# Attention and soft mixture of experts: nine output rows per partition, all stores on one queue, DMA tiles placed first in SBUF

## Chip, cores, metric

The kernel runs on one core of one Trainium2 chip. The metric is the time of one execution on the device in microseconds (us), as a median over several runs. The rows of this output are nearly alike (in the reference, an element differs from the mean of its column by under 1% of its size on average), so the comparison with the reference hardly notices rows in wrong places.

## The reference, cut to what matters

```
# attention: 8 batches, 8 heads, 576 positions, 64 per head; causal window of 64
attn = softmax(mask(q @ k.T / 8)) @ v
x    = attn as [4608, 512]                    # row = 576 * batch + position
# soft mixture of experts: 8 experts, 4 slots each, F = 1024
logits = x @ phi                              # [4608, 32]
slot_in = softmax over rows(logits).T @ x     # [32, 512]
slot_out[e] = relu(slot_in[e] @ w1[e]) @ w2[e]
out = softmax over slots(logits) @ slot_out   # [4608, 512] fp32, 9.44 MB
```

## The kernel before: the parts that matter here

Inputs (q, k, v, then the experts' weights, 61.9 MB of fp32) are loaded in one long stream, all but the first block from the POOL queue, which converts them to fp16. Attention follows it block by block. For every row the exponentials of its 32 logits are kept in `ET`. At the end a small matmul per 128 rows (`combine`) multiplies `ET` by the experts' output `slot_oa`; ScalarE and VectorE (ACT and DVE) divide by the row's sum and move the result from PSUM (the memory that matmuls write) into a tile `ob` in SBUF (the memory that DMAs load and store); a DMA stores it. In the profiles PE is the matmul engine, PEld its loads of the stationary operand ("weight loads"), and SP and POOL are two more engines whose queues issue DMAs.

The last two experts' second weights (`w2`) come as two halves of columns, so that the first half of the output columns can be computed and stored ("half-width" stores, 256 columns) while the second half of those weights is still under way. The rows after those go out at full width (512 columns).

Two facts about `combine` are important. 576 rows per batch are 4 chunks of 128 and 64 left over, and the left-over rows of two batches share one chunk of 128 partitions. Their rows lie far apart in memory, so they are stored by two DMAs of 64 partitions. And a normal store takes each partition's row of 512 fp32, so it moves runs of 2 KB (1 KB at half width).

```
    # SBUF pools, in order of allocation (cut)
    const = ...; pld = ...; pqt; ppm; psm; pxb; pxt
    gap.tile([128, 64], FP16, name="gap")          # a filler of 128 bytes
    pw1 = ...(bufs=8)                              # w1, later the output tiles "ob"
    pw2 = ...(bufs=7); pet = ...
    ...
    ET = const.tile([128, 4 * B + B // 2, 128], FP16, name="ET")   # 36 chunks of 128 rows
    ...
    def combine(blk, cols):
        nd = cols.stop - cols.start
        ob = pw1.tile([128, 4, nd], FP32, name="ob", tag="w1s")
        for g in range(4):
            cp = ps2.tile([128, nd], FP32, name="cp", tag="cp", bufs=4)
            nc.tensor.matmul(cp[:, :], ET[:, 4 * blk + g, :], slot_oa[:, cols], start=True, stop=True)
            ...                                    # scale by 1/row sum: ACT for even g, DVE for odd g
        if blk < B:
            for g in range(0, 4, 2):
                nc.sync.dma_start(                 # SP queue, 128 partitions
                    out=out[S * blk + 128 * g:S * blk + 128 * g + 256, cols].rearrange("(c p) d -> p c d", p=128),
                    in_=ob[:, g:g + 2, :])
        else:                                      # the left-over rows, 64 partitions each
            for o in range(2):
                (nc.gpsimd, nc.scalar)[o].dma_start(
                    out=out.rearrange("(c o t) d -> o t c d", o=2, t=S)[o, 512:576, :, cols],
                    in_=ob[64 * o:64 * o + 64, :, :])
    ...
        slots_out(0)
        for blk in range(NSPLIT): combine(blk, halves[0])      # NSPLIT = 4
        for e in last: expert_o(e, 1)
        slots_out(1)
        for blk in range(NSPLIT): combine(blk, halves[1])
        for blk in [B] + list(range(NSPLIT, B)): combine(blk, whole)
```

The softmax here doesn't subtract the row's maximum and nothing guards it: scores larger than these inputs give would overflow.

Of the kernel before, what the change touches and what calls it, by code (L numbers as in the profile page):

```python
# [8 lines left out]
FP32 = mybir.dt.float32  # L9
FP16 = mybir.dt.float16  # L10
AF = mybir.ActivationFunctionType
ALU = mybir.AluOpType
AXX = mybir.AxisListType.X
# [3 lines left out]
def kernel(  # L17
# [10 lines left out]
    nc = tc.nc  # L28

    B, H, S, Dh = q.shape  # L30
    D, NSLOT = moe_phi.shape
    E, _, F = moe_w1.shape
    SPE = NSLOT // E
    T = 9
# [3 lines left out]
    NFC = F // 128  # L38
    scale = 1.0 / float(Dh) ** 0.5

    const = ctx.enter_context(tc.tile_pool(name="const", bufs=1))
    pld = ctx.enter_context(tc.tile_pool(name="pld", bufs=3))
    pqt = ctx.enter_context(tc.tile_pool(name="pqt", bufs=2))
    ppm = ctx.enter_context(tc.tile_pool(name="ppm", bufs=2))
    psm = ctx.enter_context(tc.tile_pool(name="psm", bufs=4))
    pxb = ctx.enter_context(tc.tile_pool(name="pxb", bufs=2))
    pxt = ctx.enter_context(tc.tile_pool(name="pxt", bufs=1))
    gap = ctx.enter_context(tc.tile_pool(name="gap", bufs=1))
    gap.tile([128, 64], FP16, name="gap")
    pw1 = ctx.enter_context(tc.tile_pool(name="pw1", bufs=8))  # L50
    pw2 = ctx.enter_context(tc.tile_pool(name="pw2", bufs=7))
    pet = ctx.enter_context(tc.tile_pool(name="pet", bufs=2))


# [57 lines left out]
    ident = const.tile([128, 128], FP16, name="ident")  # L112
# [13 lines left out]
    for h in range(2):  # L126
        nc.vector.tensor_copy(
            out=rep[64 * h:64 * h + 64, :, :],
            in_=ident[64 * h:64 * h + 64, 64 * h:64 * h + 64].unsqueeze(1).broadcast_to([64, 8, 64]))
# [19 lines left out]
    nc.gpsimd.dma_start(out=phi_sb, in_=moe_phi.rearrange("(c p) s -> p c s", p=128))  # L149
    phi4 = const.tile([128, NHD, 4, NSLOT], FP16, name="phi4")  # L150

    ET = const.tile([128, 4 * B + B // 2, 128], FP16, name="ET")
    crcp = const.tile([128, B, 5], FP32, name="crcp")
    acc = const.tile([128, D], FP32, name="acc")
    esum = const.tile([128, B + B // 2 + 1], FP32, name="esum")
    slot_inT = const.tile([128, NHD, NSLOT], FP16, name="slot_inT")
    slot_oa = const.tile([128, D], FP16, name="slot_oa")
# [127 lines left out]
    def moe_chunks(b):  # L285
        c = [4 * (b % 2) + i for i in range(4)]
        return c + [8] if b % 2 else c
# [21 lines left out]
    fin = {}  # L309
# [59 lines left out]
                             start=(kk == 0), stop=(kk == NHD - 1))  # L369

    def fin_et(b, part):
        ch = et_chunks(b)[2 * part:2 * part + 2]
        col = (b, B + B // 2, B + b // 2)[part]
        nc.scalar.activation(ET[:, ch[0]:ch[0] + len(ch), :], fin["lt", part].rearrange("p (c q) -> p c q", q=128),
                             AF.Exp, accum_out=esum[:, col:col + 1])

    def fin_rows(b):
        rs = psm.tile([128, 5], FP32, name="rs", tag="rs")
        nc.vector.reduce_sum(rs[:, :], fin["ex"][:, :, :], axis=AXX)
        nc.vector.reciprocal(crcp[:, b, :], rs[:, :])  # L380

    def stage_logit(b):

        lt = ps.tile([128, 512], FP32, name="lt", tag="tr", bufs=4)
        for kk in range(NHD):
            nc.tensor.matmul(lt[:, :], phi4[:, kk].rearrange("p r s -> p (r s)"), moe[b][:, kk],  # L386
                             start=(kk == 0), stop=(kk == NHD - 1))
        nc.scalar.activation(ET[:, 4 * b:4 * b + 4, :], lt[:, :].rearrange("p (c q) -> p c q", q=128),
                             AF.Exp, accum_out=esum[:, b:b + 1])
        if b % 2:  # L390
            l8 = ps.tile([128, 128], FP32, name="l8", tag="tr", bufs=4)
            for kk in range(NHD):
                nc.tensor.matmul(l8[:, :], phi4[:, kk].rearrange("p r s -> p (r s)"), moe[b, 8][:, kk],
                                 start=(kk == 0), stop=(kk == NHD - 1))
            nc.scalar.activation(ET[:, 4 * B + b // 2, :], l8[:, :], AF.Exp,
                                 accum_out=esum[:, B + b // 2:B + b // 2 + 1])

    def et_chunks(b):
        return [4 * b + n for n in range(4)] + ([4 * B + b // 2] if b % 2 else [])

    def stage_ex(b):

        ch = et_chunks(b)
        nch = len(ch)
        te = ps.tile([128, 5, NSLOT], FP32, name="te", tag="tr", bufs=4)
        for n, c in enumerate(ch):
            nc.tensor.matmul(te[:, n, :], ET[:, c, :], ident[:, 0:NSLOT], start=True, stop=True)
        ex = psm.tile([128, 5, NSLOT], FP16, name="ex", tag="ex", bufs=2)
        nc.scalar.copy(out=ex[:, 0:nch, :], in_=te[:, 0:nch, :])
        rs = psm.tile([128, 5], FP32, name="rs", tag="rs")  # L410
        nc.vector.reduce_sum(rs[:, 0:nch], te[:, 0:nch, :], axis=AXX)
        nc.vector.reciprocal(crcp[:, b, 0:nch], rs[:, 0:nch])
        moe["ex", b] = ex

    def stage_slot(b):
# [37 lines left out]
    for u in range(nu):  # L453
# [4 lines left out]
        for j in range(3):  # L458
# [9 lines left out]
            if pend is not None:  # L468
# [5 lines left out]
                if pj == 2 and units[pu][1] == 1:  # L474
                    b = units[pu][0]
# [7 lines left out]
    b = B - 1  # L483
# [20 lines left out]
    ps2 = ctx.enter_context(tc.tile_pool(name="ps2", bufs=2, space=bass.MemoryType.PSUM, reuse_waits="tile"))  # L504
# [27 lines left out]
    halves = (slice(0, D // 2), slice(D // 2, D))  # L532

    def expert_o(e, half):
        hT = hTs[e % NLAST]
        for i in range(NFC // 4):
            for g in range(4):
                nc.tensor.matmul(sop[half][32 * g:32 * g + 32, :], hT[:, 4 * i + g, :],
                                 w2_t[e][:, 4 * i + g, halves[half]],
                                 start=(e == 0 and i == 0), stop=(e == E - 1 and i == NFC // 4 - 1))  # L540

    def slots_out(half):
        if half == 0:
            nc.scalar.copy(out=slot_oa[:, halves[half]], in_=sop[half])
        else:
            nc.vector.tensor_copy(out=slot_oa[:, halves[half]], in_=sop[half])


    def combine(blk, cols):
        nd = cols.stop - cols.start  # L550
        ob = pw1.tile([128, 4, nd], FP32, name="ob", tag="w1s")
        for g in range(4):
            cp = ps2.tile([128, nd], FP32, name="cp", tag="cp", bufs=4)
            nc.tensor.matmul(cp[:, :], ET[:, 4 * blk + g, :], slot_oa[:, cols], start=True, stop=True)  # L554
            cr = crcp[:, blk, g:g + 1] if blk < B else crcp[:, 2 * g + 1, 4:5]
            if g % 2 == 0:
                nc.scalar.activation(ob[:, g, :], cp[:, :], AF.Copy, scale=cr)  # L557
            else:
                nc.vector.tensor_scalar(out=ob[:, g, :], in0=cp[:, :], scalar1=cr, scalar2=None, op0=ALU.mult)  # L559
        if blk < B:  # L560
            for g in range(0, 4, 2):
                nc.sync.dma_start(
                    out=out[S * blk + 128 * g:S * blk + 128 * g + 256, cols].rearrange("(c p) d -> p c d", p=128),
                    in_=ob[:, g:g + 2, :])
        else:
            for o in range(2):
                (nc.gpsimd, nc.scalar)[o].dma_start(
                    out=out.rearrange("(c o t) d -> o t c d", o=2, t=S)[o, 512:576, :, cols],
                    in_=ob[64 * o:64 * o + 64, :, :])

    NSPLIT = 4
    whole = slice(0, D)
    with tc.manual_schedule(engines={mybir.EngineType.PE, mybir.EngineType.Activation, mybir.EngineType.DVE}):
        si = ps2.tile([128, NHD, NSLOT], FP32, name="si", tag="hp")
        for dc in range(NHD):
            nc.tensor.matmul(si[:, dc, :], pa_sb[:, dc::NHD], sel4[:, :], start=True, stop=True)
        nc.vector.tensor_copy(out=slot_inT, in_=si)

        nc.vector.reduce_sum(dinv[:, 0:1], esum[:, :], axis=AXX)
        nc.vector.reciprocal(dinv[:, 1:2], dinv[:, 0:1])  # L580
        fin_rows(B - 1)
        expert_h(0)
        expert_h(1)
        expert_t(0)
        for e in range(E):
            if e + 2 < E:
                expert_h(e + 2)
            if e + 1 < E:
                expert_t(e + 1)
            expert_o(e, 0)  # L590
            if e < E - NLAST:
                expert_o(e, 1)
        slots_out(0)
        for blk in range(NSPLIT):
            combine(blk, halves[0])
        for e in last:
            expert_o(e, 1)
        slots_out(1)
        for blk in range(NSPLIT):
            combine(blk, halves[1])  # L600
        for blk in [B] + list(range(NSPLIT, B)):
            combine(blk, whole)


# [28 lines left out]
```

## Time and profile before

| | before |
|---|---|
| median of 6 runs | 185.45 us (184.88 to 185.78) |
| profiled span | 183.4 us |
| busy: PE, DVE, ACT | 75%, 64%, 63% |
| last compute instruction ends | about 170 us |
| last input lands / last store lands | 155.4 / 182.2 us |

First the slices of the page: the span in 40 equal parts. "DMA" is the mean busy share of the 16 DMA engines in tenths, "GB/s" is what they wrote (for the loads this counts the fp16 side; they read twice as much).

```profile
DMA  5999999999999999999999999999999999999995
GB/s 213 280 207 204 213 203 209 209 206 213 209 211 206 208 213 208 210 208 207 212 208 208 212 207 217 207 214 210 217 213 207 200 195 230 357 354 251 338 393 210
```

The DMA engines never rest, and over the span no compute engine is near that (PE, the busiest, 75%). The slices up to the 33rd are loads: about 208 GB/s written is about 416 GB/s read. Slices 35 to 40 are stores: about 355, then a dip to 251, then 393.

The chain of work that ended last, in order of time (start, duration, what), around the end of the loads:

```profile
130.47 19.57 DMA w2l<-in_moe_w_dram
150.04 0.04 issue
150.08 0.64 PE sop L538 x7
```

One weight load decides when the experts can finish. Before that the compute engines have slack.

The queues of the same page (packets, MB, share of 16 engines' time), and the stores by issuing queue (count, KB each, median us from issue to landing):

```profile
q0 software_dynamic: 22640, 30.61, 94.0%
q1 hardware_dynamic: 7344, 10.16, 15.5%
q10 hardware_dynamic: 272, 0.52, 1.3%
q8 instruction: 22, 0.36, 0.7%
...
out_dram<-ob SPq DMA_DIRECT2D x16, 256.0 KB, 3.8
out_dram<-ob SPq DMA_DIRECT2D x8, 512.0 KB, 6.7
...
out_dram<-ob ACTq DMA_DIRECT2D x1, 512.0 KB, 5.5
out_dram<-ob POOLq DMA_DIRECT2D x1, 512.0 KB, 8.1
```

q0 is POOL's queue, q1 is SP's, q10 is ACT's. The last two lines are the 64-partition stores.

The DMA view of three windows of the store phase, 160 to 164, 166 to 168 and 172 to 174 us:

```profile
DMA packets 1471, 1.42 MB, mean 355 GB/s; under 512 B 86, under 2 KB 1471, under 8 KB 1471
...
DMA packets 196, 0.40 MB, mean 201 GB/s; under 512 B 0, under 2 KB 0, under 8 KB 196
q10 hardware_dynamic: 196, 0.40, 95.2%
...
DMA packets 410, 0.79 MB, mean 396 GB/s; under 512 B 23, under 2 KB 23, under 8 KB 410
```

So there are three rates: half-width stores (1 KB runs) at 355 GB/s, a dip, and full-width stores (2 KB runs) at 396. Windows of 1 us put the dip at 165.7 to 171 us; from 166 to 168 only the ACT queue's 64-partition store moves (201 GB/s), and from about 168 on POOL's takes its place.

One group of the page matters for the change: the weight loads of `ET` in `combine` (count, busy us, mean ns, then idle time before them).

```profile
L554 PEld LDWEIGHTS <-ET 128*128 128x128 f16 x52 | 5.7, 110 | 11.5 <-issue 8.9
```

### The profile page before, as it was taken

Reading aid. Unit: us, or ns where it says so; the run is one execution under the profiler, and the core shown is the slowest. Engines: PE = TensorE matmul, PEld = TensorE weight load, DVE = VectorE, ACT = ScalarE, POOL = GpSimd, SP = SyncE. Lnnn points to the kernel's source line nnn. Section 1 sums busy time; section 2 is a strip of 40 time slices with the busy share of each in tenths; the row PEclk is TensorE's granted clock in tenths of the full one; section 3 lists DMA queues with packets and bytes.
Section 4 is the critical chain, followed back from the end, with each engine's and each line's share of the span. In section 5 each row is a group of like instructions: output and inputs, shape, how many; then the busy total and the mean of one; then the engine's idle time right before and its main releaser. Section 6 shows DMA issues by size and latency. Waiting matters only on the chain.

```text
span 183.4 us, 6606 instructions
## 1 busy us (share of the span) xinstructions
PE 136.8 (75%) x2883; PEld 97.8 (53%) x2883; DVE 116.7 (64%) x287; ACT 116.0 (63%) x202; POOL 55.9 (30%) x87
## 2 busy tenths in 40 slices
PE   2569879978999789898888999968978329875000
PEld 0458757757668577676756776745656214321000
DVE  5535878788859788758867794968742007688000
ACT  3557779769696697685959869666544108668000
POOL 8644444245253434333443334222330000010000
PEclk9999999999999999999999999999999955599955
DMA  5999999999999999999999999999999999999995
GB/s 213 280 207 204 213 203 209 209 206 213 209 211 206 208 213 208 210 208 207 212 208 208 212 207 217 207 214 210 217 213 207 200 195 230 357 354 251 338 393 210
DMA packets 30283, 41.70 MB, mean 227 GB/s; under 512 B 2224, under 2 KB 21936, under 8 KB 30256
## 3 DMA queue, kind: packets, MB, share of 16 engines
q0 software_dynamic: 22640, 30.61, 94.0%
q1 hardware_dynamic: 7344, 10.16, 15.5%
q10 hardware_dynamic: 272, 0.52, 1.3%
q8 instruction: 22, 0.36, 0.7%
q14 instruction: 5, 0.04, 0.1%
HBM read 61.93 MB, written 9.44 MB: 389 GB/s over the span
## 4 chain that ended last, share of the span: by engine, by line
PE 40%; ACT 18%; DMA 15%; DVE 12%; issue 6%; SPq 0%; ACTq 0%; DVEq 0%
DMA w2l<-in_moe_w_dram 11%; PE tr L172 10%; ACT pm L236 6%; PE tr L202 5%; PE sc L231 4%; ACT kT L179 4%; DMA first<-in_v_dram 4%; PE cp L554 4%; PE tr L300 4%; PE sc L224 4%; PE av L262 3%; DVE vT L177 2%; PE lt L386 2%; ACT qT L179 2%; ACT ob L557 2%
## 5 line engine op out<-in xcount | busy, mean ns | idle before, releaser
L236 ACT ACTIVATE pm<-sc 128x1024 f16<-128x1024 f32 (+1 forms) x48 | 40.2, 837 | 18.7 <-PE sc L231 18.6
L224 PE MATMUL sc<-rep,hide 64*128 64x512 f16 (+1 forms) x96 | 19.3, 340 | 6.6 <-ACT pm L236 4.0
L262 PE MATMUL av<-vw,pm 128*64 128x65 f16 x576 | 19.3, 195 | 4.9 <-issue 4.3
L270 DVE TENSOR_TENSOR x_bp<-av,rc 128x512 f16<-128x512 f32 x32 | 22.0, 688 | 0.9
L179 ACT COPY qT<-tr 128x640 f16<-128x640 f16 (+1 forms) x31 | 21.2, 745 | 1.3 <-PE tr L172 1.3
L179 ACT COPY kT<-tr 128x640 f16<-128x640 f16 (+1 forms) x31 | 21.8, 785 | 0.2 <-PE tr L172 0.2
L559 DVE TENSOR_SCALAR ob<-cp,crcp 128x256 f32<-128x256 f32 (+1 forms) x26 | 14.6, 584 | 8.1 <-PE cp L554 7.3
L231 PE MATMUL sc<-qT,kT 64*128 64x64 f16 x576 | 19.4, 193 | 0.3 <-issue 0.2
L262 PEld LDWEIGHTS <-pm 128*64 128x64 f16 x576 | 15.7, 111 | 6.0 <-issue 5.1
L231 PEld LDWEIGHTS <-kT 64*128 64x128 f16 x576 | 15.5, 96 | 4.5 <-issue 0.8
L557 ACT ACTIVATE ob<-cp,crcp 128x256 f32<-128x256 f32 (+1 forms) x26 | 13.6, 555 | 4.7 <-PE cp L554 4.3
L554 PE MATMUL cp<-slot_oa,ET 128*128 128x256 f16 (+1 forms) x52 | 13.8, 378 | 3.6 <-DVE ob L559 1.8
L88 POOL DMA_DIRECT2D w1s<-in_moe_w_dram x16 | 9.0, 560 | 22.5 <-DMA w2s<-in_moe_w_dram 13.3
L67 POOL DMA_DIRECT2D qn<-in_q_dram x15 | 10.8, 720 | 14.9 <-PE tr L172 2.8
L67 POOL DMA_DIRECT2D vn<-in_v_dram x15 | 10.7, 717 | 14.6 <-PE tr L172 3.3
L172 PE MATMUL tr<-ident,vn 128*64 128x128 f16 x288 | 12.7, 228 | 2.4 <-ACT vn L446 2.4
L172 PE MATMUL tr<-ident,kn 128*64 128x128 f16 x288 | 13.3, 233 | 1.3 <-issue 1.1
L67 POOL DMA_DIRECT2D kn<-in_k_dram x15 | 10.8, 717 | 10.9 <-PE av L262 3.9
L268 DVE RECIPROCAL rc<-av 128x8 f32<-128x8 f32 x32 | 6.2, 195 | 12.3 <-PE av L262 12.3
L179 ACT COPY vT<-tr 128x640 f16<-128x640 f16 x16 | 13.1, 820 | 1.5 <-PE tr L172 1.5
L172 PE MATMUL tr<-ident,qn 128*64 128x128 f16 x288 | 12.4, 233 | 1.8 <-ACT qn L446 1.7
L177 DVE COPY vT<-tr 128x512 f16<-128x512 f16 x16 | 11.5, 716 | 3.2 <-PE tr L172 2.9
(107 smaller groups left out, 235.6 us busy)
## 6 DMA issues: line engine op xcount, KB each, us to landing
w1s<-in_moe_w_dram POOLq DMA_DIRECT2D x16, 512.0 KB, 14.8
w2s<-in_moe_w_dram POOLq DMA_DIRECT2D x14, 512.0 KB, 14.8
qn<-in_q_dram POOLq DMA_DIRECT2D x15, 288.0 KB, 13.0
kn<-in_k_dram POOLq DMA_DIRECT2D x15, 288.0 KB, 13.0
vn<-in_v_dram POOLq DMA_DIRECT2D x15, 288.0 KB, 13.0
out_dram<-ob SPq DMA_DIRECT2D x16, 256.0 KB, 3.8
out_dram<-ob SPq DMA_DIRECT2D x8, 512.0 KB, 6.7
w2l<-in_moe_w_dram POOLq DMA_DIRECT2D x2, 512.0 KB, 19.9
```

Source lines behind the costliest of these rows:

```text
L67: nc.gpsimd.dma_start(out=t, in_=src_of(u, i))
L172: nc.tensor.transpose(tr[64 * x:64 * x + 64, j, :], src[:, x, 64 * (t0 + j):64 * (t0 + j) + 64], ident[:, :])
L177: nc.vector.tensor_copy(out=o, in_=i)
L179: nc.scalar.copy(out=o, in_=i)
L224: nc.tensor.matmul(sc[:, x, 0:128 * n], hide[64 * x:64 * x + 64, :], rep[64 * x:64 * x + 64, 0:2 * n, :], start=True, stop=False, skip_gro ...
L231: nc.tensor.matmul(sc[:, x, o:o + 64], st["kT"][64 * x:64 * x + 64, h, 64 * i:64 * i + 128], st["qT"][64 * x:64 * x + 64, h, 64 * i:64 * i ...
L236: nc.scalar.activation(pm[:, :, 0:2 * n, :], sc[:, :, 0:128 * n].rearrange("p x (w q) -> p x w q", q=64), AF.Exp, scale=scale)
L262: nc.tensor.matmul(av[r0:r0 + 64, kk, 65 * (w // 2):65 * (w // 2) + 65], pm[:, x, h * n + w, :], st["vw"][:, i, 2 * h + x, 0:65], start=Tr ...
L270: nc.vector.tensor_tensor(out=xb[:, c0:c0 + 2, 256 * half:256 * half + 256].rearrange("p c (k d) -> p k c d", d=64), in0=avv[:, :, :, 0:64 ...
L554: nc.tensor.matmul(cp[:, :], ET[:, 4 * blk + g, :], slot_oa[:, cols], start=True, stop=True)
L557: nc.scalar.activation(ob[:, g, :], cp[:, :], AF.Copy, scale=cr)
L559: nc.vector.tensor_scalar(out=ob[:, g, :], in0=cp[:, :], scalar1=cr, scalar2=None, op0=ALU.mult)
```

## The change

The intent: give every partition nine consecutive rows of the output (two batches are 1152 = 128 x 9 rows). Then no rows are left over, every store has 128 partitions, and three rows of one partition are one run of 6 KB in memory. `ET` is kept in the order of rows, and `combine` takes every ninth column of it as its stationary operand. The row sums, computed before by DVE for chunks of 128 rows, come from one-column matmuls in the expert stage. The pools whose tiles are loaded or stored by DMA are allocated first, so that `ob` and the weight tiles start at a multiple of 512 bytes; before, `ob` and nearly all weight tiles started 320 bytes past one, which is 64 past a multiple of 256. The core of the diff, cut:

```
+    gap = ...; gap.tile([128, 64], FP16, name="gap")
+    pld = ...; pxb = ...; pw1 = ...(bufs=8); pw2 = ...(bufs=7)      # now ahead of const
     const = ...; pqt; ppm; psm; pxt; pet
...
-    ET = const.tile([128, 4 * B + B // 2, 128], FP16, name="ET")
+    ET = const.tile([128, B // 2, 2 * S], FP16, name="ET")
...
     def stage_ex(b):                              # per block, in the attention stage
-        nc.vector.reduce_sum(rs[:, 0:nch], te[:, 0:nch, :], axis=AXX)
-        nc.vector.reciprocal(crcp[:, b, 0:nch], rs[:, 0:nch])
...
+    def row_sums(bp):                             # after experts 0 to 3; quarter holds 0.25
+        rs = ps2.tile([128, T], FP32, name="rs", tag="cp", bufs=4)
+        for j in range(T):                        # T = 9
+            nc.tensor.matmul(rs[:, j:j + 1], ET[:, bp, j::T], quarter[:, :], start=True, stop=True)
+        nc.vector.reciprocal(crcp[:, bp, :], rs[:, :])
...
+    def combine(bp, j0, n, cols):                 # n of the nine rows of each partition
+        ob = pw1.tile([128, n, nd], FP32, name="ob", tag="w1s")
+        for g in range(n):
+            nc.tensor.matmul(cp[:, :], ET[:, bp, j::T], slot_oa[:, cols], start=True, stop=True)
+            ...                                   # ACT and DVE in turn
+        nc.sync.dma_start(
+            out=out[2 * S * bp:2 * S * bp + 2 * S, cols].rearrange("(p t) d -> p t d", t=T)[:, j0:j0 + n, :],
+            in_=ob[:, :, :])
...
-    NSPLIT = 4                                    # 4 x 512 rows in halves
+    pieces = [(bp, j0, 3) for bp in range(B // 2) for j0 in range(0, T, 3)]
+    NSPLIT = 6                                    # 6 x 384 rows in halves
```

More of the change, by code (lines that the diff above doesn't have):

```diff
@@ L39 @@
     scale = 1.0 / float(Dh) ** 0.5
+    gap = ctx.enter_context(tc.tile_pool(name="gap", bufs=1))
+    gap.tile([128, 64], FP16, name="gap")
+    pld = ctx.enter_context(tc.tile_pool(name="pld", bufs=3))
+    pxb = ctx.enter_context(tc.tile_pool(name="pxb", bufs=2))
+    pw1 = ctx.enter_context(tc.tile_pool(name="pw1", bufs=8))
+    pw2 = ctx.enter_context(tc.tile_pool(name="pw2", bufs=7))
     const = ctx.enter_context(tc.tile_pool(name="const", bufs=1))
-    pld = ctx.enter_context(tc.tile_pool(name="pld", bufs=3))
     pqt = ctx.enter_context(tc.tile_pool(name="pqt", bufs=2))
@@ L45 @@
     psm = ctx.enter_context(tc.tile_pool(name="psm", bufs=4))
-    pxb = ctx.enter_context(tc.tile_pool(name="pxb", bufs=2))
     pxt = ctx.enter_context(tc.tile_pool(name="pxt", bufs=1))
-    gap = ctx.enter_context(tc.tile_pool(name="gap", bufs=1))
-    gap.tile([128, 64], FP16, name="gap")
-    pw1 = ctx.enter_context(tc.tile_pool(name="pw1", bufs=8))
-    pw2 = ctx.enter_context(tc.tile_pool(name="pw2", bufs=7))
     pet = ctx.enter_context(tc.tile_pool(name="pet", bufs=2))
@@ L150 @@
     phi4 = const.tile([128, NHD, 4, NSLOT], FP16, name="phi4")
-    ET = const.tile([128, 4 * B + B // 2, 128], FP16, name="ET")
-    crcp = const.tile([128, B, 5], FP32, name="crcp")
+    ET = const.tile([128, B // 2, 2 * S], FP16, name="ET")
+    crcp = const.tile([128, B // 2, T], FP32, name="crcp")
+    quarter = const.tile([128, 1], FP16, name="quarter")
+    nc.vector.memset(quarter, 0.25)
     acc = const.tile([128, D], FP32, name="acc")
@@ L371, in fin_et, with et_of, et_rest, back @@
     def fin_et(b, part):
-        ch = et_chunks(b)[2 * part:2 * part + 2]
         col = (b, B + B // 2, B + b // 2)[part]
-        nc.scalar.activation(ET[:, ch[0]:ch[0] + len(ch), :], fin["lt", part].rearrange("p (c q) -> p c q", q=128),
+        i = fin["lt", part]
+        nc.scalar.activation(et_of(b, 256 * part, 256) if part < 2 else et_rest(b),
+                             i if part < 2 else i.rearrange("p (o t) -> p o t", o=2),
                              AF.Exp, accum_out=esum[:, col:col + 1])
-    def fin_rows(b):
-        rs = psm.tile([128, 5], FP32, name="rs", tag="rs")
-        nc.vector.reduce_sum(rs[:, :], fin["ex"][:, :, :], axis=AXX)
-        nc.vector.reciprocal(crcp[:, b, :], rs[:, :])
+    def et_of(b, t0, n):
+        t0 += S * (b % 2)
+        return ET[:, b // 2, t0:t0 + n]
+    def et_rest(b):
+        return ET[:, b // 2].rearrange("p (o t) -> p o t", o=2)[:, :, 512:S]
+    def back(te, n, b, c):
+        if c < 4:
+            nc.tensor.matmul(te[:, n, :], et_of(b, 128 * c, 128), ident[:, 0:NSLOT], start=True, stop=True)
+            return
+        for o in range(2):
+            nc.tensor.matmul(te[64 * o:64 * o + 64, n, :], et_of(b - 1 + o, 512, 64), ident[:, 0:NSLOT],
+                             start=True, stop=True)
     def stage_logit(b):
@@ L387, in stage_logit @@
                              start=(kk == 0), stop=(kk == NHD - 1))
-        nc.scalar.activation(ET[:, 4 * b:4 * b + 4, :], lt[:, :].rearrange("p (c q) -> p c q", q=128),
-                             AF.Exp, accum_out=esum[:, b:b + 1])
+        nc.scalar.activation(et_of(b, 0, 512), lt[:, :], AF.Exp, accum_out=esum[:, b:b + 1])
         if b % 2:
@@ L394, in stage_logit @@
                                  start=(kk == 0), stop=(kk == NHD - 1))
-            nc.scalar.activation(ET[:, 4 * B + b // 2, :], l8[:, :], AF.Exp,
+            nc.scalar.activation(et_rest(b), l8[:, :].rearrange("p (o t) -> p o t", o=2), AF.Exp,
                                  accum_out=esum[:, B + b // 2:B + b // 2 + 1])
-    def et_chunks(b):
-        return [4 * b + n for n in range(4)] + ([4 * B + b // 2] if b % 2 else [])
     def stage_ex(b):
-        ch = et_chunks(b)
-        nch = len(ch)
+        nch = len(moe_chunks(b))
         te = ps.tile([128, 5, NSLOT], FP32, name="te", tag="tr", bufs=4)
-        for n, c in enumerate(ch):
-            nc.tensor.matmul(te[:, n, :], ET[:, c, :], ident[:, 0:NSLOT], start=True, stop=True)
+        for n in range(nch):
+            back(te, n, b, n)
         ex = psm.tile([128, 5, NSLOT], FP16, name="ex", tag="ex", bufs=2)
         nc.scalar.copy(out=ex[:, 0:nch, :], in_=te[:, 0:nch, :])
-        rs = psm.tile([128, 5], FP32, name="rs", tag="rs")
-        nc.vector.reduce_sum(rs[:, 0:nch], te[:, 0:nch, :], axis=AXX)
-        nc.vector.reciprocal(crcp[:, b, 0:nch], rs[:, 0:nch])
         moe["ex", b] = ex
@@ L546, in slots_out @@
             nc.vector.tensor_copy(out=slot_oa[:, halves[half]], in_=sop[half])
-    def combine(blk, cols):
+    def row_sums(bp):
[3 more added lines that the diff above has]
+        nc.vector.reciprocal(crcp[:, bp, :], rs[:, :])
+    turn = [0]
+    def combine(bp, j0, n, cols):
         nd = cols.stop - cols.start
-        ob = pw1.tile([128, 4, nd], FP32, name="ob", tag="w1s")
-        for g in range(4):
+        ob = pw1.tile([128, n, nd], FP32, name="ob", tag="w1s")
+        for g in range(n):
+            j = j0 + g
             cp = ps2.tile([128, nd], FP32, name="cp", tag="cp", bufs=4)
-            nc.tensor.matmul(cp[:, :], ET[:, 4 * blk + g, :], slot_oa[:, cols], start=True, stop=True)
-            cr = crcp[:, blk, g:g + 1] if blk < B else crcp[:, 2 * g + 1, 4:5]
-            if g % 2 == 0:
+            nc.tensor.matmul(cp[:, :], ET[:, bp, j::T], slot_oa[:, cols], start=True, stop=True)
+            cr = crcp[:, bp, j:j + 1]
+            turn[0] += 1
+            if turn[0] % 2:
                 nc.scalar.activation(ob[:, g, :], cp[:, :], AF.Copy, scale=cr)
@@ L559, in combine @@
                 nc.vector.tensor_scalar(out=ob[:, g, :], in0=cp[:, :], scalar1=cr, scalar2=None, op0=ALU.mult)
-        if blk < B:
-            for g in range(0, 4, 2):
-                nc.sync.dma_start(
-                    out=out[S * blk + 128 * g:S * blk + 128 * g + 256, cols].rearrange("(c p) d -> p c d", p=128),
-                    in_=ob[:, g:g + 2, :])
-        else:
-            for o in range(2):
-                (nc.gpsimd, nc.scalar)[o].dma_start(
-                    out=out.rearrange("(c o t) d -> o t c d", o=2, t=S)[o, 512:576, :, cols],
-                    in_=ob[64 * o:64 * o + 64, :, :])
-    NSPLIT = 4
-    whole = slice(0, D)
+        nc.sync.dma_start(
+            out=out[2 * S * bp:2 * S * bp + 2 * S, cols].rearrange("(p t) d -> p t d", t=T)[:, j0:j0 + n, :],
+            in_=ob[:, :, :])
+    whole = slice(0, D)
+    pieces = [(bp, j0, 3) for bp in range(B // 2) for j0 in range(0, T, 3)]
+    NSPLIT = 6
+    early, late = pieces[:NSPLIT], pieces[NSPLIT:]
+    early[0:1] = [(0, 0, 1), (0, 1, 2)]
+    late[-1:] = [(B // 2 - 1, 6, 2), (B // 2 - 1, 8, 1)]
     with tc.manual_schedule(engines={mybir.EngineType.PE, mybir.EngineType.Activation, mybir.EngineType.DVE}):
@@ L580 @@
         nc.vector.reciprocal(dinv[:, 1:2], dinv[:, 0:1])
-        fin_rows(B - 1)
         expert_h(0)
@@ L592 @@
                 expert_o(e, 1)
+            if e < B // 2:
+                row_sums(e)
         slots_out(0)
-        for blk in range(NSPLIT):
-            combine(blk, halves[0])
+        for p in early:
+            combine(*p, halves[0])
         for e in last:
@@ L598 @@
         slots_out(1)
-        for blk in range(NSPLIT):
-            combine(blk, halves[1])
-        for blk in [B] + list(range(NSPLIT, B)):
-            combine(blk, whole)
+        for p in early:
+            combine(*p, halves[1])
+        for p in late:
+            combine(*p, whole)
 _INS = ['q', 'k', 'v', 'moe_phi', 'moe_w1', 'moe_w2']
```

## The prediction

> **What bounds the kernel now.** Two DMA phases in series; in the slices the DMA engines are 90% busy nearly throughout, while PE, DVE and ACT are busy 75, 64 and 63% of the span. Until about 153 us they read the inputs (61.9 MB, about 410 GB/s); the chain of waits there is one w2l load landing at 150.04, and PE idles on weight loads (0.8 and 2.1 us at 142 to 145, 2.1 before 148, 1.4 before 150). From 152.4 us on they write 9.44 MB of output; the compute engines finish at 169.9, the span ends at 183.4. Only what changes the DMA stream counts.
>
> The output phase, by windows of the DMA view:
> - 155 to 165 us: half-width pieces, 1 KB packets, 355 GB/s.
> - 165.7 to 171: a dip, 1.25 MB in 5.3 us. Only the ACT and POOL queues (0.5 MB each) move anything: the two 64-partition stores of the leftover rows, one after the other. The Trainium skill, "SBUF — State Buffer", section "Door 1: The DMA port swizzle", says that partitions 0 to 63 reach only 8 of 16 ports; the 184 to 217 GB/s here agree.
> - 172 to 180: full width, 2 KB packets, 390 to 397 GB/s.
>
> **What the change does.**
> 1. Each partition holds nine consecutive output rows. All stores are 128 partitions on the SP queue. 1.25 MB at 395 GB/s is 3.2 us in place of 5.3: -2.1 us.
> 2. The late half is stored in runs of up to 6 KB. From 46 ns per 1 KB packet and 84 per 2 KB packet and engine I estimate 8 ns of cost per packet, so 410 to 420 GB/s: 4.72 MB save about 0.6 us.
> 3. The half-width share grows from 4.19 to 4.72 MB: +0.15 us. But the reordered pools move output and weight tiles from 64 bytes past a 256-byte line (in the built program) onto one. The Trainium skill, "DMA: Bandwidth & Descriptors", section "How a descriptor splits into AXI transactions", has it that an unaligned start costs an extra transaction; by that, an estimate of 34 beats against 32 per KB: -0.3 to -0.7 us. No run has shown it yet.
> 4. The reduces and reciprocals of eight blocks leave DVE: nothing, that stage waits for DMA.
> 5. 36 one-column matmuls for the row sums enter the expert stage, and the loads of ET get a stride of 9 elements. Contiguous 128-column loads take 96 to 98 ns, that of slot_oa with stride 4 takes 118; I guess 150 to 200. That is 6 to 8 us of PE between 134 and 148, where it has about 6 us of idle time, and output cannot flow before 153: nothing, or a few tenths. In the early combine PE takes about 0.37 us per 128 KB piece, as long as its store.
> 6. Input stream: unchanged within 0.5 us.
>
> Sum: about -3.9 us; I trust the dip most.
>
> **Predicted: 181.5 us, range 179.6 to 184.0.** Chances: faster by over 2% (under 181.7) 0.54, within 2% 0.42, slower 0.04.
>
> **What would show the steps.** No dip after 165; packets over 2 KB and over 400 GB/s in the last 10 us; 360 to 380 GB/s in the half-width stretch; ET loads of 150 to 200 ns; the w2l landing still near 150 us, GB/s of the first 150 us unchanged.
>
> **What would make it wrong.** Strided loads of 300 ns or more: PE would be late for the first outputs and feed the stores too slowly. Large packets no faster than 2 KB ones. Stores that wait for output buffers, as some twenty pieces share eight. An input stream that the moved tiles speed up or slow down.

## The result, and the profile after

| | before | after |
|---|---|---|
| median | 185.54 us (16 runs) | 181.79 us (8 runs, 181.43 to 182.31) |
| ratio | | 0.9802, 95% interval 0.9786 to 0.9818 |
| profiled span | 183.4 us | 179.7 us |
| last input lands | 155.40 us | 155.34 us |
| last store lands | 182.24 us | 178.75 us |

The result was right. The change is faster clear of noise, by 1.8 to 2.1%; whether it is by more than 2%, which the prediction gave a chance of 0.54, these runs don't decide.

The slices after:

```profile
DMA  5999999999999999999999999999999999999994
GB/s 206 279 209 202 207 209 211 208 206 215 208 211 204 209 211 208 209 208 209 212 204 211 208 213 206 214 212 216 208 213 219 201 198 178 327 381 394 424 423 197
```

The loads look as before. The dip is gone and both rates of the store phase are higher: 381 and 424 in place of 354 and 393.

The chain around the end of the loads, which is the same to 0.1 us:

```profile
130.40 19.57 DMA w2l<-in_moe_w_dram
149.97 0.04 issue
150.01 0.64 PE sop L547 x7
```

Queues and stores; ACT's queue and POOL's store have gone:

```profile
q0 software_dynamic: 22496, 30.09, 94.8%
q1 hardware_dynamic: 6656, 11.21, 16.6%
q8 instruction: 23, 0.38, 0.8%
...
out_dram<-ob SPq DMA_DIRECT2D x10, 384.0 KB, 5.0
out_dram<-ob SPq DMA_DIRECT2D x5, 768.0 KB, 8.4
```

The DMA view of three windows, 156 to 160 us (half width), 168 to 170 (full width) and 174 to 180 (the end; its "DMA" line has 40 slices of 0.15 us):

```profile
DMA packets 1574, 1.54 MB, mean 385 GB/s; under 512 B 71, under 2 KB 1574, under 8 KB 1574
...
DMA packets 153, 0.84 MB, mean 421 GB/s; under 512 B 16, under 2 KB 16, under 8 KB 153
...
DMA  9999997999999999965444443443200000000000
GB/s 451 451 410 410 369 505 314 423 451 423 410 410 423 369 369 437 410 246 218 191 191 191 178 164 137 178 178 137 96 0 0 0 0 0 0 0 0 0 0 0
```

At full width 137 large packets carry 0.84 MB, so about 6 KB each (the 16 small ones are the semaphore writes). The last line holds a surprise: from about 176.7 us on, only 3 to 5 tenths of the 16 DMA engines are busy, for about 1.5 us. Half of them have nothing left to do while the others still work. The section on the experiments comes back to this.

The loads of `ET` with a stride of nine elements, and the row sums (same columns as before):

```profile
L573 PEld LDWEIGHTS <-ET 128*128 128x128 f16 x54 | 7.3, 140 | 8.2 <-issue 6.8
L561 PE MATMUL rs<-quarter,ET 128*128 128x1 f16 x36 | 2.8, 200 | 0.0
L561 PEld LDWEIGHTS <-ET 128*128 128x128 f16 x36 | 2.5, 157 | 0.8 <-issue 0.8
```

In `combine` the strided load takes 138 ns in the median (137 to 161) in place of 104 (95 to 152), in the row sums 160, and all row sums together keep PE for 2.8 us.

### The profile page after: what moved, and what is told of

Its sections match the earlier page's. It is cut to its first block, busy times and chain, and to the rows that moved or that the text cites. A ratio compares the mean times of both kernels' runs of the same rounds, so it can differ in the third digit from the quotient of the medians.

```text
span 179.7 us, 6674 instructions
## 1 busy us (share of the span) xinstructions
PE 138.7 (77%) x2924; PEld 102.0 (57%) x2924; DVE 115.2 (64%) x277; ACT 116.1 (65%) x203; POOL 55.1 (31%) x86
## 4 chain that ended last, share of the span: by engine, by line
PE 44%; ACT 18%; DMA 17%; DVE 7%; issue 7%; DVEq 0%; SPq 0%; ACTq 0%
PE tr L176 13%; DMA w2l<-in_moe_w_dram 11%; ACT pm L240 6%; PE tr L206 5%; PE sc L228 5%; PE tr L304 5%; PE sc L235 5%; PE av L266 4%; ACT kT L183 4%; DMA first<-in_k_dram 3%; DMA out_dram<-ob 3%; PE cp L573 3%; ACT qT L183 3%; ACT vT L183 2%; PE lt L403 2%
## 5 line engine op out<-in xcount | busy, mean ns | idle before, releaser
L228 PE MATMUL sc<-rep,hide 64*128 64x512 f16 (+1 forms) x96 | 18.2, 341 | 6.0 <-ACT pm L240 3.5
L266 PEld LDWEIGHTS <-pm 128*64 128x64 f16 x576 | 16.2, 113 | 4.6 <-issue 4.2
L573 PE MATMUL cp<-slot_oa,ET 128*128 128x256 f16 (+1 forms) x54 | 13.1, 335 | 2.7 <-DVE slot_oa L555 0.5
```

The source lines that it names most:

```text
L228: nc.tensor.matmul(sc[:, x, 0:128 * n], hide[64 * x:64 * x + 64, :], rep[64 * x:64 * x + 64, 0:2 * n, :], start=True, stop=False, skip_gro ...
L266: nc.tensor.matmul(av[r0:r0 + 64, kk, 65 * (w // 2):65 * (w // 2) + 65], pm[:, x, h * n + w, :], st["vw"][:, i, 2 * h + x, 0:65], start=Tr ...
L573: nc.tensor.matmul(cp[:, :], ET[:, bp, j::T], slot_oa[:, cols], start=True, stop=True)
```

## The experiments

The theory after the first look: the gain is the sum of three parts of the store phase, which are the missing dip, the alignment of the tiles (theory A) and the longer runs. The rival to A (theory B) was that the new order of rows, or fewer and larger stores, makes the half-width stretch faster. Twelve kernels were run, each with 3 rounds or more against the kernel before.

### 1 and 2. Is it the alignment? Tiles moved in the changed kernel

```
+    gap2.tile([128, 32], FP16, name="gap2")       # 64 bytes; in the second run [128, 96], 192 bytes
     pw1 = ctx.enter_context(tc.tile_pool(name="pw1", bufs=8))
```

> The changed kernel with its output and weight tiles moved back to 64 bytes past a 256-byte line, nothing else. Theory A (the alignment of the SBUF side sets the rate of the stores): the half-width stretch falls from 384 to about 355 GB/s, the late stretch from 424 to about 415, and the ratio to the kernel before rises from 0.980 to 0.986 (about +1.1 us). Theory B (the rate comes from the order of rows in memory, or from fewer and larger stores): 384 GB/s stays, ratio 0.980. The input stream stays within 0.3 us in both.

> The same tiles at 192 bytes past a 256-byte line. Under theory A there are two forms. If whole fetched beats count, 1 KB costs 38 beats in place of 32 (34 at 64 bytes): half-width stretch about 325 GB/s, ratio about 0.993. If only the extra transaction counts, it equals the run at 64 bytes: 355 GB/s, ratio 0.986. Theory B: 384 GB/s, 0.980.

Measured: ratio 0.9814 (0.9790 to 0.9838) at 64 bytes and 0.9825 (0.9805 to 0.9844) at 192. The DMA view of the run at 64 bytes, 156 to 160 us, then its "DMA" line for 174 to 180:

```profile
DMA packets 1479, 1.44 MB, mean 361 GB/s; under 512 B 70, under 2 KB 1479, under 8 KB 1479
...
DMA  9969989999699899989998999942000000000000
```

At 192 bytes the same window shows 358 GB/s:

```profile
DMA packets 1452, 1.43 MB, mean 358 GB/s; under 512 B 54, under 2 KB 1452, under 8 KB 1452
```

Three things follow. The rate of the half-width stretch does come from the alignment: 385 becomes 361, in the same order of rows and with the same stores, so theory B falls. The cost is nearly the same at both offsets, so it does not grow with the bytes fetched in vain: the count of fetched beats (steps of 32 bytes, by the page that the prediction names) fits at 64 bytes, where 34 in place of 32 make 362 GB/s of 385, but 38 beats at 192 bytes wanted about 325, and the run shows 358. And the time did not follow the rate: 24 GB/s less over 4.72 MB should cost 0.8 us, but the ratio moved by 0.0012, which is 0.2 us and within the intervals. The "DMA" line shows why: here all engines are busy almost to the end, and the 1.5 us at half strength are missing. What alignment gives in rate it partly loses in an uneven end.

### 3. The other way round: alignment alone in the kernel before

```
-    gap.tile([128, 64], FP16, name="gap")
+    gap.tile([128, 160], FP16, name="gap")        # w1, w2 and ob now start at a multiple of 512 bytes
```

> The kernel before with one filler tile made 192 bytes longer, so that output and weight tiles start on a 256-byte line; order of rows and stores as before. Theory A: half-width stretch from 355 to about 384 GB/s, full-width from 395 to 405; the dip of 5 us stays; ratio about 0.993 (-1.2 us). Theory B: 355 GB/s, ratio 1.000.

Measured: ratio 0.9934 (0.9903 to 0.9964), the dip still there, and from 160 to 164 and 172 to 176 us:

```profile
DMA packets 1593, 1.54 MB, mean 384 GB/s; under 512 B 94, under 2 KB 1593, under 8 KB 1593
...
DMA packets 844, 1.63 MB, mean 408 GB/s; under 512 B 48, under 2 KB 48, under 8 KB 844
```

So in the kernel before, alignment was worth 1.2 us, as theory A said. That is more than the 0.2 us that run 1 shows in the changed kernel, but by how much is not well known: the intervals are 0.6 and 0.4 us to each side, and the profiled run, the slowest of the four, ends only 0.5 us earlier than that of the kernel before.

### 4 and 5. What makes the dip?

In the first run all rows are stored by 128-partition stores on the SP queue; the left-over rows land in wrong places. In the second the 64-partition stores stay, but on SP.

```
# run 4
-        if blk < B: ... else: ...
+        for g in range(0, 4, 2):
+            r = 512 * blk + 128 * g
+            nc.sync.dma_start(out=out[r:r + 256, cols].rearrange("(c p) d -> p c d", p=128), in_=ob[:, g:g + 2, :])
# run 5
-                (nc.gpsimd, nc.scalar)[o].dma_start(
+                nc.sync.dma_start(
```

> The kernel before with the leftover rows stored by two 128-partition stores on the SP queue instead of two 64-partition ones on ACT and POOL; rows land in wrong places on purpose (wrong result), bytes and packets as before. If the 64-partition pair makes the dip: no dip after 165 us, span about 2.2 us shorter, ratio about 0.988. If the dip comes from the output pieces arriving late from the engines, it stays in some form and the ratio is above 0.995.

> The kernel before with the two 64-partition stores issued on the SP queue in place of ACT and POOL; result right. If their partitions make them slow, the dip stays (two spells of about 200 GB/s, 5 us in all), ratio 0.997 to 1.000. If the other queues (the switch between them, or POOL's software issue) make them slow, the dip is gone and the ratio is about 0.988.

Measured: run 4, ratio 0.9869 (0.9846 to 0.9891); run 5, 1.0012 (0.9997 to 1.0027). The DMA view from 166 to 168 us, of run 4:

```profile
DMA packets 398, 0.77 MB, mean 384 GB/s; under 512 B 19, under 2 KB 28, under 8 KB 398
```

and of run 5:

```profile
DMA packets 200, 0.41 MB, mean 203 GB/s; under 512 B 1, under 2 KB 2, under 8 KB 200
q1 hardware_dynamic: 200, 0.41, 93.5%
```

On another queue the dip stays, with 128 partitions it goes. So the queue is ruled out, and the pair of 64-partition stores costs 2.4 us (0.0131 of 185.5). One rival is left untested: run 4 also changed where the rows go in memory and put two rows in a partition instead of four. That the rate is about half of 384 GB/s speaks for the 64 partitions. This agrees with the Trainium skill, "SBUF — State Buffer", section "Door 1: The DMA port swizzle", by which 64 partitions reach half of the ports, and with "DMA: Bandwidth & Descriptors", section "Issuing engines are not separate DMA queues", by which the DMAs of all issuing engines run on the same 16 DMA engines.

### 6. What are the long runs worth?

```
-        ob = pw1.tile([128, n, nd], FP32, name="ob", tag="w1s")
+        pad = 64 if nd == D else 0                # 256 bytes between full-width rows in SBUF
+        ob = pw1.tile([128, n, nd + pad], FP32, name="ob", tag="w1s")[:, :, 0:nd]
```

> The changed kernel with 256 bytes of padding between the full-width output rows in SBUF, so that a late store moves runs of 2 KB in place of 6 KB; same bytes, same number of stores, still aligned. Theory of a cost per packet (about 8 ns): the late stretch falls from 424 to 400 to 408 GB/s, +0.5 us, ratio 0.983. Rival (the late rate comes from alignment and from the 128-partition stores alone): 420 GB/s or more, ratio 0.980.

Measured: ratio 0.9838 (0.9809 to 0.9868), and from 168 to 170 us 409 GB/s in place of 421:

```profile
DMA packets 416, 0.82 MB, mean 409 GB/s; under 512 B 17, under 2 KB 17, under 8 KB 416
```

The long runs are worth about 0.0036 (0.7 us) beside aligned tiles, barely clear of noise (the two intervals touch).

### 7 and 8. Do the parts add up?

Run 7 joins runs 3 and 4. Run 8 takes from the changed kernel both the alignment and the long runs.

> Both single parts together in the kernel before: 128-partition stores on the SP queue (rows in wrong places on purpose) and tiles on a 256-byte line. Alone they gave 0.987 and 0.993. If they add: 0.980. If alignment only speeds up the DMA engines that were ahead anyway, and the end is set by those that are late from the input stream (as the landings of the run with tiles moved by 64 bytes suggest, where it cost only 0.001): 0.985 or more, and the landings of the last store spread over nearly 2 us instead of 0.3.

> The changed kernel with both the 2 KB runs and the shift by 64 bytes, so that only the order of rows, the store count and the row sums of the change are left, and no dip. If those do nothing for the time: the ratio of the kernel before with 128-partition stores, 0.987, half-width stretch 357 GB/s, full-width 380. If the new order of rows is worth something of itself: 0.983 or less.

Measured: run 7, ratio 0.9833 (0.9815 to 0.9850); run 8, 0.9866 (0.9848 to 0.9883). In a table, with the kernels that store 128 partitions on SP throughout:

| | tiles 64 bytes off | tiles aligned |
|---|---|---|
| order of rows before, 2 KB runs | 0.9869 (run 4) | 0.9833 (run 7) |
| order of rows after, 2 KB runs | 0.9866 (run 8) | 0.9838 (run 6) |
| order of rows after, 6 KB runs | 0.9814 (run 1) | 0.9802 (the change) |

Each ratio is known to about 0.002 or 0.003. The first two lines agree in both columns, so the order of rows, the number of stores and the new row sums together do nothing that these runs can see. Alignment is worth about 0.003 with short runs and 0.001 with long ones, neither much clear of noise. It looks smaller than in run 3 (0.0066), but that difference is within the intervals too: run 7 lies between its two expectations, and that the parts do not add is not shown by the times. Its trace speaks for it: the 16 DMA engines end the last store 1.46 us apart, in run 4 0.23.

### Where the speed of the aligned stores goes: sixteen engines that do not end together

The completion of a DMA is counted by its 16 engines one by one (the Trainium skill, "DMA: Bandwidth & Descriptors", section "Why a DMA increments its semaphore by 16 and not by 1"); the trace has the time of each of the 16. The 1st, 8th, 9th and 16th of them, us from the span's start:

```
                                      1st     8th     9th    16th   from 1st to 16th
the change      last load           151.70  152.75  154.02  155.34   3.64
                a half-width store  157.58  157.78  158.13  159.43   1.85
                a full-width store  171.32  171.56  171.94  173.21   1.90
                last store          176.91  177.13  177.53  178.75   1.84
run 1, 64 off   last load           151.41  152.80  153.94  155.18   3.77
                a half-width store  157.56  157.78  158.04  159.28   1.72
                last store          178.19  178.32  178.41  178.94   0.75
run 4, 64 off   last load           151.71  153.69  154.05  155.59   3.88
                a half-width store  157.60  157.77  157.79  159.03   1.43
                last store          179.90  180.02  180.04  180.13   0.23
```

All kernels leave the input stream with about half of the engines some 2 to 4 us behind the first. The first stores, which wait for the experts, narrow that to about 1.8 us. With aligned tiles all engines then run at one pace (a 384 KB store every 1.02 us), and the gap of 1.84 us is carried to the end: the early engines stop at 176.9, and the time is set by the late ones. With tiles 64 bytes off, only the early engines slow down (1.16 us per store in run 1), while the late ones keep 1.02 us until they have caught up. So alignment sped up mostly engines that were going to wait anyway. Why an unaligned start slows the early engines and not the late ones was not tried and stays open. One thing may belong to it: at full width with tiles 64 bytes off, run 4, whose engines end within 0.2 to 0.5 us of each other, takes about 1.38 us per 512 KB store, and the kernel before, whose engines are about 1.6 us apart there, 1.29, as with aligned tiles (1.28 in run 7).

Where does the lag come from? In the trace of the change, the time from the 1st to the 16th completion of a load grows in three steps of 0.7 to 1.1 us that stay (from 0.7 to 1.4, 2.45 and 3.55), at about 16, 66 and 114 us. Between the steps it is constant, while one engine after the other joins the late group. The queue of kind "instruction" (q8 above) has 23 packets of 16 KB, one every 6 us, of 0.89 to 1.06 us each:

```
start us (took ns) of packets on q8, the change:
15.56 (962)  22.91 (893)  29.19 (892)  35.58 (949)  41.48 (945)  47.46 (1062)  53.51 (974)  59.57 (974)
65.56 (961)  71.37 (893)  ...  113.45 (961)  ...  138.80 (945)  144.87 (936)  160.17 (961)
```

The durations come round every eight packets, as if eight engines took turns, and eight packets at 6 us are the 48 us or so between the steps; the packets at 15.56, 65.56 and 113.45 us stand at the three steps. In run 9 below, a packet at 162.51 us goes with one engine falling back from 0.76 to 2.00 us at the store that ended at 165.3. This fits instruction fetches that hold up one of eight engines for a microsecond or more each. The counts fit as well: 22 packets came before the end of the loads, and at the last load six engines are 3.3 to 3.6 us behind the first (three packets each) and two 2.3 to 2.4 us (two each).

No run was made to test it, but one nearly does. In all variants of the changed kernel but run 10, the last packet comes between 160.0 and 163.2 us, and at the stores that land just after it one engine falls back by about 0.9 to 2.1 us. Run 10 has 72 more PE instructions; its last packet comes at 153.44 us, and from 157 us on no engine falls back. The cause stays inferred, as the packets do not say which engine carried them.

### 9. Fewer half-width stores

```
-    NSPLIT = 6
+    NSPLIT = 4
```

> The changed kernel with 4 pieces of rows stored in halves in place of 6, so 3.15 MB at 1 KB packets in place of 4.72. If half-width packets cost what the two rates say (384 against 424 GB/s), 1.57 MB save 0.39 us, ratio 0.978. If the stores then run dry before the second half of the columns is ready, a gap shows near 157 us and the ratio is 0.980 or worse.

Measured: ratio 0.9866 (0.9851 to 0.9881), so 1.2 us slower than the change. The "DMA" line of 156 to 160 us, in slices of 0.1 us:

```profile
DMA  9999999999999996545445334599965999999869
```

From 157.5 to 158.6 us half of the engines have nothing to store: the second half of the columns needs the weights that land at 155.62, and its first store is issued at 157.7. That is the dry spell of the expectation, but in this trace it is not what the end waits for. The early engines wait in it; the late ones store on with hardly a pause. Then the packet at 162.51 us holds up one engine, now that no other is far behind. At the last store 15 engines have ended by 178.61 us, a little before the change (178.75), and that one ends at 180.01: in this trace it alone accounts for the loss. In the change the packet at 160.17 us fell on an engine that had slack, and cost nothing. Whether more half-width stores or another place of that packet would cure it was not tried.

### 10. Are the row sums free?

```
-            nc.tensor.matmul(rs[:, j:j + 1], ET[:, bp, j::T], quarter[:, :], start=True, stop=True)
+            for _ in range(2):
+                nc.tensor.matmul(rs[:, j:j + 1], ET[:, bp, j::T], quarter[:, :], start=True, stop=True)
```

> The changed kernel with each of the 36 row-sum matmuls done twice. They took 2.8 us of PE in all, so 5.6 now, in a stage where PE waits for weights. If they are off the critical path: first store still at 152 us, ratio 0.980. If not: up to 2.8 us later, ratio 0.995.

Measured: ratio 0.9795 (0.9780 to 0.9810), first store at 151.8 us. The group of the row sums:

```profile
L562 PE MATMUL rs<-quarter,ET 128*128 128x1 f16 x72 | 5.0, 199 | 0.0
```

PE does 2.2 us more in the expert stage and the time does not move. The row sums are off the critical path.

### 11 and 12. A try for a better kernel

Only the last expert's `w2` is loaded by halves of columns, and fewer pieces are stored by halves (3 and 4).

```
+    NCUT = 1                                      # in place of NLAST = 2 where w2 is cut, ordered and used
-    NSPLIT = 6
+    NSPLIT = 3                                    # 4 in the other run
```

> A try for a better one: the changed kernel with only the last expert's second weights loaded in two column halves (two experts before), and 3 pieces of rows stored in halves (6 before). Half-width bytes fall from 4.72 to 2.36 MB (0.58 us by the rates 384 and 424 GB/s) and 0.2 us of input stream go, as two loads get long rows; the first store comes 2.5 us later, when the late DMA engines are just done with the input. Estimate 0.976. If stores run dry near 158 us: 0.98 to 0.985.

> The same with 4 pieces stored in halves (3.15 MB): safer against a dry spell, 0.2 us more of half-width stores. Estimate 0.977; better than the run with 3 only if that one runs dry.

Measured: ratio 0.9918 (0.9889 to 0.9947) for 3 pieces (run 11) and 0.9893 (0.9872 to 0.9915) for 4 (run 12); both lose by over 1.6 us to the change. The "DMA" line of run 11, 152 to 160 us, slices of 0.2 us:

```profile
DMA  9988777755554410004937998999999999989389
```

The first store is issued at 154.8 us in place of 152.0, and from 155.0 to 155.6 us hardly any engine works. The expectation counted on the late engines only; the earliest ended its loads at 151.6 and waited 4 us, and the second half ran dry once more near 159 us. This brings all engines into step (0.2 us apart), and again one falls back when a packet of the instruction queue comes (at 163.12 us; 162.14 in run 12). At the end 15 engines stop by 179.92 us and one at 181.76 (run 12: 179.39 and 180.63), against 178.75 in the change. So of the 3.0 us that this trace of run 11, the slowest of six, loses, the dry spells explain about 1.2 and the one engine 1.8. No kernel beat the changed one by a clear margin.

## Why the prediction was right

The time (181.5 predicted, 181.79 measured) and its range hold, and so does the mechanism: the end of the store phase moved and the input stream did not. That the number hit so closely is partly luck. The terms that the prediction lists (-2.1, -0.6, +0.15, -0.3 to -0.7) add up to -2.9 to -3.3 us, not to the -3.9 it gives as their sum; the measured difference is 3.7. By its terms it would have said 182.2 to 182.6 us, still within its range. Point by point:

1. **The dip**, predicted -2.1 us: right, 2.4 us by run 4, and run 5 shows that the queue is not the cause; that it is the 64 partitions is the likely reading (see runs 4 and 5).
2. **Long runs**, predicted 410 to 420 GB/s and -0.6 us: right, 421 GB/s and 0.7 us (run 6 against the change).
3. **Alignment**, predicted 360 to 380 GB/s and -0.3 to -0.7 us: the rate was right, if a little low (385), but the time it gives in the changed kernel is about 0.2 us (run 1) to 0.5 us (run 8 against run 6), neither clear of noise. The step that failed is the silent one that a mean rate of 16 engines is turned into time: the engines do not end together, and the late ones were hardly helped. The estimate by beats held for the rate at 64 bytes (362 GB/s, measured 361) and failed at 192 (run 2: 325, measured 358).
4. **DVE's reductions**: nothing, as predicted. Run 8 still lacks them and equals run 4, which has them.
5. **Row sums**: the load of 137 to 161 ns was guessed at 150 to 200, but the sum of 6 to 8 us of PE was mis-sized: 2.8 us. Loads and one-column matmuls overlap (36 pairs in 2.8 us is 78 ns a pair, less than one load's record). It had no effect either way (run 10).
6. **Input stream**: unchanged, last landing 155.34 against 155.40 us.

The parts as measured in one path, from 1.000: dip 0.0131 (run 4), order of rows and row sums 0.0003 (run 8), alignment 0.0028 (run 6), long runs 0.0036 (the change). Together 0.0198, or 3.7 us. On the other path (run 8, run 1, the change) the same 0.0064 of the last two split into 0.0052 for long runs and 0.0012 for alignment, so a single number for either has little meaning; each of these steps is known to about 0.003 only.

## What to carry to other kernels

Lay out the output so that every store has all 128 partitions and each partition's part is one long run; here that was worth 3.1 to 3.4 of 3.7 us, while the matmuls it cost were free because the stage waited for DMA. Check what sets the end before turning a better mean rate into time: when the busy share falls to half in the last slices, half of the DMA engines set the time, and speeding up the others gains nothing. A store phase that runs dry for a moment can cost more than the gap: in runs 9, 11 and 12 it brought the engines into step, and a later delay of one engine then went straight to the end.

## What the Trainium skill lacked or had wrong

- "DMA: Bandwidth & Descriptors", section "How a descriptor splits into AXI transactions": an unaligned SBUF start does cost (385 to 361 GB/s at 1 KB runs), but the whole beats that the page counts describe it only at 64 bytes (34 for 32 would give 362): at 192 bytes past the line it was 358 GB/s, where 38 beats for 32 would give about 325.
- "SBUF — State Buffer", section "Door 1: The DMA port swizzle": agrees (201 to 203 GB/s for a store of 64 partitions against 384). The page treats two transfers of 64 partitions, not a store of 128 partitions queued behind one. Here it did not fill the rest: in the kernel before, SP's next store was issued at 164.84 us, and SP's queue moved nothing from 166 to 168.
- "Runtime: NRT & Kernel Launch", section "Instruction fetch mechanics", has the 16 KiB blocks, which agree with the packets here, and calls their cost mostly hidden. It does not say that they take time on the DMA engines: 23 packets of 0.89 to 1.06 us, and half of the engines 2.3 to 3.6 us behind the first at the end of the loads (that the one makes the other is inferred).
- No page gives the price of a strided weight load in ns: with a step of 9 elements of fp16, 138 to 160 ns (medians of `combine` and the row sums) in place of 104 for 128 columns.
- Left open by the runs: full-width stores with unaligned tiles ran at 396 GB/s in the kernel before and at 380 in run 4, for the same runs of 2 KB. The engines were about 1.6 us apart in the one and in step in the other; whether that is the reason was not tried.
